# A two-layer spectral and MLP kernel on one core: layer 2's transform over d by frequency modulo four, W left in order, the transform back in halves, copies split by PSUM bank

## The chip, the core and the metric

The kernel runs on one core of one Trainium2 chip. Its engines work side by side, each through its own queue in program order: TensorE (PE; its weight loads are PEld) multiplies into PSUM, VectorE (DVE) and ScalarE (ACT) copy out of PSUM and do the elementwise work, GpSimd (POOL) does small arithmetic on statistics and issues some loads, and SyncE (SP) issues the other DMAs. PSUM has eight banks of 512 fp32 columns. The metric is device microseconds of one launch, the median of several runs.

## The reference

Two layers, each A then B, every one on a normalised input and added back to x, which is 2048 x 512 in bf16.

```
def _A_ref(x, w_r, w_i):
    X = jnp.fft.rfft2(x.astype(jnp.float32), axes=(-2, -1))
    X = X * (w_r + 1j * w_i)
    return jnp.fft.irfft2(X, s=(S, D), axes=(-2, -1)).astype(jnp.bfloat16)

def _B_ref(x, w1, w2, w3, w4):
    h = _gelu(_layernorm(x) @ w1)
    # four column groups of h, moved by 1, -1, 2, -2 rows, zero padded
    x1 = x + shifted(h) @ w2
    return x1 + _gelu(_layernorm(x1) @ w3) @ w4

x = A_x
for _ in range(2):
    x = x + _A_ref(_layernorm(x), A_w_r, A_w_i)
    x = x + _B_ref(_layernorm(x), B_w1, B_w2, B_w3, B_w4)
return x
```

(Here the two layers are written as a loop and the shifts as one name.) D is 512, the hidden width of w3 is 1792.

## The kernel before

The rows are held as s = 16 p + q: 128 partitions p, sixteen row groups q, so that x_state, of 128 x 16 x 512, stays in SBUF for the whole launch. A spectral part goes through these steps, all of them matrix products with tables of sines and cosines:

- *Front* (O, then G): for each q a product over p. The table T is first scaled by the row's 1/std into a tile Tq (Q); TensorE multiplies x_state by it (over_p, over_p_quarters or over_p_plain), and the result is put into V. The sum and the difference of columns d and d+256 serve the even and the odd frequencies; sums of sums and differences of sums serve frequencies 0 and 2 modulo 4. Layer 1's front, over_p_quarters, makes all four parts inside the product, in 8 matmuls a row. Layer 2's front has two ways: for the first PLAIN = 5 pairs of rows, over_p_plain takes 4 matmuls of 128 columns a row and fold_V makes sums and differences on VectorE from the result and from a copy ("right") that ScalarE makes; the others go through over_p, 4 matmuls of 256 columns. Neither makes the sums of sums.
- *Forward*: over_d (d) transforms over d, block by block (16 blocks b, mostly two to a unit u); take_d (t) copies into a tile TV; over_q (q) transforms over q in 64-row matmuls; take_q (x) copies to X, a tile with two buffers; weigh (p) multiplies by the filter W on VectorE; back_q (b) goes back over q, one PSUM bank a block; take_b (m) copies into M, which lies in hT.
- *Back*: back_d (D) goes back over d from all blocks, both halves F of the frequencies summed in one go; take_D (Y) copies; back_p (P) goes back over p; add_x (a) adds to x_state and sums; stats2 (s) squares on ScalarE; rstd2, std_twice, invert_twice and ratio (r, e, i, c) make the scale; norm2 (n) normalises into xn; tr (T) has SyncE transpose xn by DMA into xT.

Layer 1's over_d works with the table FL: two matmuls of 128 columns (frequencies 0 and 2 modulo 4) and two of 256 (the odd ones) a block, and take_d scatters the columns by four. Layer 2's over_d has the table FA and four matmuls of 256 columns a block, with frequencies split by parity only. For that, between the two uses, the filter W is put into even and odd halves: permute (L, sixteen times two copies on VectorE, lines 813 and 814), and G, the table of the way back, is overwritten by G2.

The MLP part is w1 (v), gelu (h), the shifted w2 (u), add_x1 (f), norm (k, R, o), transposes (U), w3 (w), gelu (g), w4 (W), add_x2 (A). In layer 1 it is interleaved with the statistics (B, j, S, J), the scaled tables (Q) and the front of layer 2; in layer 2 with the stores (y).

The order is written out by hand: ORDER_0 for layer 1's front, ORDER_A and ORDER_B for what the two layers do after it. A word such as `d15.7` is operation d on unit 15 with PSUM bank 7 as its first; a last letter A or V names the engine. Every engine runs its own words in the order of the text. `X4.0` is four filler matmuls on zeros in bank 0; WAKE = 27 fillers stand at the start. Loads of weights and tables stand in load_all.

Of the kernel before, what the change touches and what calls it, by code (L numbers as in the profile page):

```python
# [16 lines left out]
P = 128  # L17
# [11 lines left out]
def dft_tables():  # L29
# [27 lines left out]
    FA = np.stack([cos, -sin], axis=1).reshape(2, P, 2, P, 2)[..., ::-1].transpose(1, 0, 4, 2, 3)  # L57
# [8 lines left out]
    G = G.transpose(2, 0, 1)  # L66
    G2 = G.reshape(P, 2, 2, D // 2)
    G = G.reshape(2, P, 2, D // 2).transpose(1, 0, 2, 3)
# [30 lines left out]
    out = {"T": np.stack([T, -T], axis=1), "FA": FA, "FL": FL, "TL": TL, "TL2": TL2, "TR": TR, "G": G, "G2": G2,  # L99
# [9 lines left out]
def kernel(  # L109
# [30 lines left out]
    for last in (False, True):  # L140
        layer(K, last)
        if not last:
            K.load_G2()
# [18 lines left out]
def load_all(K, A_x, A_w_r, A_w_i, B_w1, B_w2, B_w3, B_w4):  # L162
# [29 lines left out]
    def load_tables():  # L192
        spare = K.grp.tile([P, 4, 4, P], BF16, name="xT", bufs=4)
        K.FL = spare[:, 0:2].rearrange("p a b c -> p (a b c)")[:, 0:768]
        K.dummy = spare[:, 2, 0:1]
        q.dma_start(K.FL, dram["FL"])
        load_TL(0)
        load_TL(1)
        load_TR(0)
# [14 lines left out]
    def load_G2():  # L214
        for f in range(2):
            nc.sync.dma_start(K.G[:, f], dram["G2"][:, f])

    K.load_G2 = load_G2

    def load_mlp():  # L220
        gate2 = K.const.tile([1, 16], BF16, name="gate2")
        nc.sync.dma_start(gate2[:], K.W[1:2, 1, NH - 1, 1:17])
        for k in ("G", "Tinv"):
            table(k, nc.sync)
        for k, w, n, c in (("w1", B_w1, 4, D), ("w2", B_w2, 4, D), ("w3", B_w3, 4, FH), ("w4", B_w4, 14, D)):
            t = K.const.tile([P, n, c], BF16, name=k)
            nc.sync.dma_start(t[:], w.rearrange("(t p) n -> p t n", p=P))
            setattr(K, k, t)
        K.FA = K.const.tile(list(tabs["FA"].shape), BF16, name="FA")
        for t in range(2):  # L230
            nc.sync.dma_start(K.FA[:, t], dram["FA"][:, t])

# [48 lines left out]
class Stats:  # L281
# [68 lines left out]
    def invert_twice(self):  # L350
        self.K.nc.vector.reciprocal(self.r[:], self.sd[:])
        self.shift()
# [34 lines left out]
    def apply(self, i, src, dst, eng):  # L387
        r = self.r[:, i:i + 1]
        if eng == "V":
            self.K.nc.vector.tensor_scalar(dst, src, self.mv[:, i, 0:1], r, op0=ALU.add, op1=ALU.mult)  # L390
# [4 lines left out]
def scaled_T(K, q, r, eng="V"):  # L395

    K.Tq[q] = K.stream.tile([P, 2, P], BF16, name="Tq", bufs=12)
# [7 lines left out]
def over_p(K, qs, split=False):  # L405

    ps = banks(K, 2 if split else len(qs))
    for i, q in enumerate(qs):
        Tq = K.Tq.pop(q)
        for t in range(2):  # L410
            o = ps[:, t, 0:256] if split else ps[:, i, t * 256:(t + 1) * 256]
            a, z = t * P, 256 + t * P
            K.nc.tensor.matmul(o, lhsT=K.x[:, q, a:a + P], rhs=Tq[:, 0:1].to_broadcast([P, 2, P]), start=True,
                               stop=False)
            K.nc.tensor.matmul(o, lhsT=K.x[:, q, z:z + P], rhs=Tq[:], start=False, stop=True)
    return ps


def over_p_quarters(K, qs, split=False):

    ps = banks(K, 2 if split else len(qs))
    for i, q in enumerate(qs):
        T = K.Tq.pop(q)
        plus, both, swap = T[:, 0], T[:], T[:, ::-1]
        twice = lambda k: T[:, k:k + 1].to_broadcast([P, 2, P])
        for h in range(2):
            o = (ps[:, h, 0:256] if split else ps[:, i, h * 256:(h + 1) * 256]).rearrange("d (k p) -> d k p", k=2)
            terms = ((0, o, twice(0)), (1, o[:, 1], plus), (3, o[:, 1], plus), (2, o, swap)) if h == 0 else \
                    ((1, o, swap), (0, o[:, 0], plus), (2, o[:, 0], plus), (3, o, twice(1)))
            for n, (c, dst, rhs) in enumerate(terms):  # L430
                K.nc.tensor.matmul(dst, lhsT=K.x[:, q, c * P:(c + 1) * P], rhs=rhs, start=(n == 0), stop=(n == 3))  # L431
    return ps
# [13 lines left out]
def fold_V(K, qs, ps, right):  # L446
    n, lo = len(qs), qs[0]
    v = K.V[:].rearrange("d (t h) b q c -> d h t q b c", h=2)[:, :, :, lo:lo + n]
    left = ps[:, :, 0:256].rearrange("d q (t b c) -> d t q b c", t=2, c=4)
    right = right.rearrange("d q (t b c) -> d t q b c", t=2, c=4)  # L450
    for h, op in ((0, ALU.add), (1, ALU.subtract)):
        for t in range(2):
            K.nc.vector.tensor_tensor(v[:, h, t], left[:, t], right[:, t], op=op)


def take_V(K, qs, ps, eng, part=False):

    dst = K.V[:].rearrange("d t b q c -> d (t b) q c")[:, :, qs[0]:qs[-1] + 1:max(qs[-1] - qs[0], 1)]
    if part:
        t = "AV".index(eng)  # L460
        dst, ps = dst[:, 64 * t:64 * t + 64], ps[:, t:t + 1, 0:256]
    copy(K, dst, ps.rearrange("d q (tb c) -> d tb q c", c=4), eng)
# [7 lines left out]
def first_front(K):  # L470
# [30 lines left out]
    def front(k):  # L501
        ps[k] = over_p_quarters(K, FIRST[k], k == len(FIRST) - 1)
# [3 lines left out]
    def take(k, eng):  # L506
        take_V(K, FIRST[k], ps[k], eng, k == len(FIRST) - 1)

    def means(g):
# [3 lines left out]
        if g == TABLES:  # L513
# [3 lines left out]
             "J": lambda g: L[g].invert(), "p": lambda g: L[g].rstd(), "Q": scale, "O": front, "G": take}  # L517
    for op in ORDER_0.split():
        if op[0] in "QG":
            table[op[0]](int(op[1:-1]), op[-1])  # L520
        else:
            table[op[0]](int(op[1:]))
    K.load_rest(last_T[:])
    K.load_mlp()
    K.nc.sync.dma_start_transpose(K.dummy, K.zeros[:])


def layer(K, last):
# [13 lines left out]
    def over_d(u):  # L542
        bs = UNITS[u]
        ps["d", u] = o = banks(K, len(bs))
        for i, b in enumerate(bs):
            if not last:
                oi = o[:, i].rearrange("p (e r f) -> p e r f", e=2, r=4)
                part = lambda k: V[:, k, 2 * b:2 * b + 2].rearrange("d b q c -> d (b q c)")
                nc.tensor.matmul(oi[:, :, 3], lhsT=part(1), rhs=K.FL[:, 0:P].rearrange("p (e f) -> p e f", e=2),
                                 start=True, stop=True)  # L550
                nc.tensor.matmul(oi[:, :, 1], lhsT=part(2), rhs=K.FL[:, P:2 * P].rearrange("p (e f) -> p e f", e=2),
                                 start=True, stop=True)
                for k in range(2):
                    rhs = K.FL[:, (k + 1) * 256:(k + 2) * 256].rearrange("p (e r f) -> p e r f", e=2, r=2)
                    nc.tensor.matmul(oi[:, :, 0:3:2], lhsT=part(3 * k), rhs=rhs, start=(k == 0), stop=(k == 1))
                continue
            oi = o[:, i].rearrange("p (e h f) -> p h e f", e=2, h=2)
            for h in range(2):
                for t in range(2):
                    nc.tensor.matmul(oi[:, 1 - h], rhs=K.FA[:, t, h],  # L560
                                     lhsT=V[:, 2 * t + h, 2 * b:2 * b + 2].rearrange("d b q c -> d (b q c)"),
                                     start=(t == 0), stop=(t == 1))

    def take_d(u, eng):
        n = len(UNITS[u])
        tv[u] = K.stream.tile([P, n, 512], BF16, name="TV", tag="TV_Y", bufs=4, padded_shape=[P, 2, 512])
        src = ps.pop(("d", u))
        if last:
            copy(K, tv[u][:], src, eng)
        else:  # L570
            copy(K, tv[u][:].rearrange("p n (e f r) -> p (n e) f r", e=2, r=4),
                 src.rearrange("p n (e r f) -> p (n e) f r", e=2, r=4), eng)
# [14 lines left out]
    def take_q(u, eng):  # L587
        n = len(UNITS[u])
        X[u] = K.stream.tile([P, 4, 256], BF16, name="X", bufs=2)
# [3 lines left out]
    def weigh(u):  # L593
        n = len(UNITS[u])
        small = n == 1 and u not in LATE[last]
        k = n_pab[small]
        n_pab[small] += 1
        if small:
            t = PB[k % 2][:, 6].rearrange("p (l h) f -> p l h f", l=2)
        else:  # L600
            t = PB[k % 2][:, 2 * (k % 6 // 2):2 * (k % 6 // 2) + 2, 0:2 * n]
        pab[u] = t
        nc.vector.tensor_tensor(t, X.pop(u)[:, 0:2 * n].unsqueeze(1).to_broadcast([P, 2, 2 * n, 256]),  # L603
                                K.W[:, :, 2 * u:2 * u + 2 * n, 1:257], op=ALU.mult)

    def back_q(b):
        u = [u for u in UNITS if b in UNITS[u]][0]
        both = TAKE_B[last][b] == "B"
        ps["b", b] = o = banks(K, 1 + both)
        for F in range(2):  # L610
            for h in range(2):
                oh = o[:, F, h * P:(h + 1) * P] if both else o[:, 0, (2 * h + F) * P:(2 * h + F + 1) * P]
                for k in range(2):
                    nc.tensor.matmul(oh,  # L614
                                     lhsT=pab[u][:, k, 2 * (b - u) + h, F * P:(F + 1) * P],
                                     rhs=K.TR[:, k:k + 2, 2 * b + h], start=(k == 0), stop=(k == 1))

    def take_b(b, eng):
        dst = M[:, :, :, :, b * 8:b * 8 + 8].rearrange("f F e q (h c) -> f h (F e) q c", h=2)
        if TAKE_B[last][b] == "B":  # L620
            F = "VA".index(eng)
            dst, src = dst[:, :, 2 * F:2 * F + 2], ps["b", b][:, F, 0:256]
        else:
            src = ps["b", b][:, 0]
        copy(K, dst, src.rearrange("f (h g q c) -> f h g q c", h=2, q=NQ, c=4), eng)

    def back_d(m):
        ps["D", m] = o = banks(K, 2)
        for F in range(2):
            for i in range(2):  # L630
                for e in range(2):
                    nc.tensor.matmul(o[:, i, e * 256:(e + 1) * 256], lhsT=M[:, F, e, 2 * m + i, :], rhs=K.G[:, F, e, :],  # L632
                                     start=(F == 0 and e == 0), stop=(F == 1 and e == 1))
# [4 lines left out]

    def back_p(q):
        ps["P", q] = o = banks(K, 1)[:, 0]  # L640
        y = Y[q // 2][:, q % 2]
        for h, e, c in ((0, 0, 0), (0, 1, 0), (1, 0, 0), (1, 1, 1)):
# [289 lines left out]
```

## Time and profile before

| | |
|---|---|
| median of 3 runs | 347.33 us (347.32 to 347.7) |
| span of the profiled execution | 345.6 us, 5672 instructions |
| granted TensorE clock | 1.00 throughout |
| HBM read and written | 12.13 MB and 2.10 MB, 41 GB/s over the span |
| w3 matmuls (L735), 448 of 512 columns | 99.3 us |
| w4 matmuls (L755) | 98.3 us |
| layer 2's over_d (L560), 64 of 256 columns | 7.7 us |
| layer 1's over_d (L549, L551, L555), 16 + 16 + 32 | 3.5 + 3.5 + 5.6 us, partly side by side |
| copies that permute W (L813, L814) | 11.0 + 6.9 us |
| fold_V (L453), 20 of 256 columns | 7.0 us |

Busy times are unions: where a matmul is drawn as 272 ns and the next starts 109 ns later, the two overlap in the record. What a matmul costs its queue is therefore read from start to start, not from its own length. Windows are counted from the start of the span.

### The profile page before, as it was taken

The numbers are of one execution on the slowest core, as the hardware profiler recorded it, in microseconds if no ns is written. First come the engines' busy times: TensorE is split into PE (matmuls) and PEld (weight loads), VectorE is DVE, ScalarE is ACT, GpSimd is POOL, SyncE is SP. The second block draws the span as 40 slices with busy tenths as digits, with TensorE's granted clock in tenths as the row PEclk, the third lists the DMA queues.
The fourth block names the chain that finished last, engine by engine and source line by source line (L and its number), as shares of the span: only waits on it lengthen the run. The fifth ranks groups of instructions, "written<-read, shape, count | busy, mean of one in ns | idle before, by whom it ended". The sixth has DMA issues, their size and how long they took to land.

```text
span 345.6 us, 5672 instructions
## 1 busy us (share of the span) xinstructions
PE 336.6 (97%) x2161; PEld 190.3 (55%) x2178; DVE 187.5 (54%) x448; ACT 195.5 (57%) x348; POOL 62.8 (18%) x157
## 2 busy tenths in 40 slices
PE   6999999999999999999999999999999999999996
PEld 4978884444444444444577888544444444444443
DVE  5989597668354351178789969757514110211021
ACT  4989899755616616015527979976572344132500
POOL 1460047530301400010000002554014001000000
PEclk9999999999999999999999999999999999999999
DMA  7997975430031210300000002572103060203012
GB/s 259 280 361 236 383 173 101 84 62 0 3 61 21 33 24 14 49 13 1 2 0 2 2 2 44 99 97 41 27 2 61 0 108 0 46 14 95 0 32 76
DMA packets 45834, 25.12 MB, mean 73 GB/s; under 512 B 35008, under 2 KB 42816, under 8 KB 45808
## 3 DMA queue, kind: packets, MB, share of 16 engines
q1 hardware_dynamic: 44336, 20.27, 24.8%
q0 software_dynamic: 1232, 4.40, 3.7%
q8 instruction: 17, 0.28, 0.4%
q10 hardware_dynamic: 240, 0.10, 0.1%
q14 instruction: 9, 0.07, 0.1%
HBM read 12.13 MB, written 2.10 MB: 41 GB/s over the span
## 4 chain that ended last, share of the span: by engine, by line
PE 83%; ACT 7%; DVE 5%; DMA 3%; issue 2%; SPq 0%; ACTq 0%; DVEq 0%
PE ps L735 28%; PE ps L755 28%; PE ps L700 8%; PE ps L684 7%; PE ps L431 3%; PE ps L632 2%; PE ps L614 2%; ACT xn L306 2%; PE ps L644 1%; ACT hT L159 1%; DVE PB L603 1%; PE ps L584 1%; ACT X L159 1%; DVE X L157 1%; DVE x_state L652 1%
## 5 line engine op out<-in xcount | busy, mean ns | idle before, releaser
L742 ACT ACTIVATE gT<-ps 128x1024 bf16<-128x1024 f32 x56 | 56.6, 1023 | 80.4 <-PE ps L735 79.7
L735 PE MATMUL ps<-xT,w 128*128 128x512 bf16 x448 | 99.3, 379 | 0.0
L755 PE MATMUL ps<-w,gT 128*128 128x512 bf16 (+1 forms) x464 | 98.3, 366 | 0.6
L755 PEld LDWEIGHTS <-gT 128*128 128x128 bf16 x476 | 46.5, 98 | 50.1
L735 PEld LDWEIGHTS <-w 128*128 128x128 bf16 x448 | 43.8, 98 | 52.6
L761 DVE TENSOR_TENSOR x_state<-ps,x_state 128x512 bf16<-128x512 f32 (+1 forms) x34 | 22.1, 657 | 86.1 <-PE ps L755 78.9
L708 DVE SCALAR_TENSOR_TENSOR xn<-xn,ln_c,ps 128x512 bf16<-128x512 bf16 x32 | 23.5, 745 | 26.3 <-PE ps L700 19.5
L700 PE MATMUL ps<-w,hT 128*128 128x512 bf16 x123 | 28.8, 379 | 0.3
L684 PE MATMUL ps<-xT,w 128*128 128x512 bf16 x128 | 28.8, 379 | 0.2 <-DMA xT<-xn 0.2
L306 ACT ACTIVATE junk<-xn 128x512 bf16<-128x512 bf16 x32 | 19.9, 622 | 12.7 <-DVE xn L708 12.7
L652 DVE SCALAR_TENSOR_TENSOR x_state<-ps,x_state 128x512 bf16<-128x512 f32 x32 | 20.5, 686 | 4.2 <-PE ps L644 4.1
L294 DVE BATCH_NORM_STATS2 ln_st<-x_state 128x6 f32<-128x512 bf16 (+1 forms) x31 | 20.1, 663 | 3.7 <-DMA x_state<-in_A_x_dram 3.5
L700 PEld LDWEIGHTS <-hT 128*128 128x128 bf16 x128 | 12.4, 98 | 15.3 <-ACT hT L691 0.8
L684 PEld LDWEIGHTS <-w 128*128 128x128 bf16 x128 | 12.3, 98 | 15.3 <-DMA xT<-xn 1.4
L312 POOL TENSOR_SCALAR ln_mv<-ln_s 128x4 f32<-128x4 f32 x16 | 5.7, 357 | 80.3 <-DVE x_state L652 68.7
L306 ACT ACTIVATE xn<-x_state 128x512 bf16<-128x512 bf16 x32 | 20.0, 631 | 0.4 <-DVE x_state L652 0.2
L603 DVE TENSOR_TENSOR PB<-X,W 128x2048 bf16<-128x2048 bf16 (+1 forms) x20 | 19.4, 1010 | 0.2
L691 ACT ACTIVATE hT<-ps 128x512 bf16<-128x512 f32 x32 | 17.4, 604 | 2.5 <-PE ps L684 2.4
L314 POOL TENSOR_TENSOR ln_mv<-ln_s,ln_t 128x4 f32<-128x4 f32 x16 | 3.8, 239 | 80.1 <-ACT junk L306 73.5
L614 PE MATMUL ps<-TR,PB 128*128 128x128 bf16 x256 | 16.3, 219 | 0.1
L159 ACT ACTIVATE TV<-ps 128x1024 bf16<-128x1024 f32 (+1 forms) x16 | 14.2, 914 | 3.8 <-PE ps L560 2.3
L644 PE MATMUL ps<-Y,Tinv 128*128 128x256 bf16 x128 | 15.4, 272 | 0.5 <-ACT Y L159 0.2
(96 smaller groups left out, 388.3 us busy)
## 6 DMA issues: line engine op xcount, KB each, us to landing
w<-in_B_w_dram SPq DMA_DIRECT2D x2, 1792.0 KB, 13.0
W<-W POOLq DMA_DIRECT2D x4, 514.0 KB, 4.7
x_state<-in_A_x_dram SPq DMA_DIRECT2D x8, 256.0 KB, 4.5
out_dram<-x_state SPq DMA_DIRECT2D x15, 128.0 KB, 1.8
w<-in_B_w_dram SPq DMA_DIRECT2D x2, 512.0 KB, 4.8
W<-in_A_w_r_dram SPq DMA_DIRECT2D x7, 128.5 KB, 6.9
W<-in_A_w_i_dram SPq DMA_DIRECT2D x7, 128.5 KB, 6.6
TL<-tab_TL POOLq DMA_DIRECT2D x3, 256.0 KB, 5.1
```

What stands on the lines that cost most here:

```text
L159: K.nc.scalar.activation(dst, src, ACT.Copy, bias=0.0, scale=1.0)
L306: K.nc.scalar.activation(out, src, ACT.Square, bias=0.0, scale=D ** -0.5, accum_out=self.s[:, i, 1:2])
L603: nc.vector.tensor_tensor(t, X.pop(u)[:, 0:2 * n].unsqueeze(1).to_broadcast([P, 2, 2 * n, 256]), K.W[:, :, 2 * u:2 * u + 2 * n, 1:257], op ...
L614: nc.tensor.matmul(oh, lhsT=pab[u][:, k, 2 * (b - u) + h, F * P:(F + 1) * P], rhs=K.TR[:, k:k + 2, 2 * b + h], start=(k == 0), stop=(k == 1))
L652: nc.vector.scalar_tensor_tensor(K.x[:, q, :], ps.pop(("P", q)), 1.0, K.x[:, q, :], op0=ALU.mult, op1=ALU.add, accum_out=ln[g].s[:, i, 0:1])
L684: nc.tensor.matmul(o[:, i], lhsT=K.w1[:, t, j * P:(j + 1) * P], rhs=xT[g][:, :, t, :], start=(t == 0), stop=(t == 3))
L700: nc.tensor.matmul(o, lhsT=K.hT[:, j, st:st + P], rhs=K.w2[:, j, :], start=(j == 0), stop=(j == 3))
L708: nc.vector.scalar_tensor_tensor(xn[:, q, :], xn[:, q, :], ln[q // 4].c[:, q % 4:q % 4 + 1], ps.pop(("u", n)), op0=ALU.mult, op1=ALU.add, ...
L735: nc.tensor.matmul(o[:, i], lhsT=K.w3[:, c, t * P:(t + 1) * P], rhs=xT3[g][:, :, c, :], start=(c == 0), stop=(c == 3))
L742: nc.scalar.activation(gT[g][:, 2 * j:2 * j + 2, :], ps.pop(("w", k)), ACT.Gelu_apprx_tanh, bias=0.0, scale=1.0)
L755: nc.tensor.matmul(o, lhsT=gT[g][:, t, i * P:(i + 1) * P], rhs=K.w4[:, t, d], start=(t == 0), stop=(t == 13))
L761: nc.vector.tensor_tensor(x, ps.pop(("W", n)), x, op=ALU.add)
```

## The change

The four-part form of V, FL and the untouched W and G now serve both layers. Layer 2's over_d takes layer 1's four matmuls; FA, G2, permute and over_p are gone, and FL has a tile of its own. Layer 2's fold_V writes the two odd parts and a tile "pairs" of sums, and fold_again makes the other two parts from it. Six pairs of rows go the plain way in place of five; pair 6 and the single rows 14 and 15 go through over_p_quarters. That function now gives one PSUM bank to each half of d and interleaves the rows of a pair in it, so that a copy can take one bank (words G and L for the halves 0 and 1).

On the way back, back_q and take_b of blocks 12 to 15 are split by F into two banks (b and V, m and l), and back_d into its two halves (D and C). X has three buffers, Tq eight in place of twelve. shift is taken out of invert_twice (M). The additions of resid, the products of weigh and the scaling of Tq can name an engine. half_D and fold_D are added; FOLD, which selects them in back_p, is empty, and the words K and H are in no order. All three orders are new; their stages are given below where they begin and end.

```diff
@@ over_p_quarters
-    ps = banks(K, 2 if split else len(qs))
+    n = len(qs)
+    ps = banks(K, 2)
     for i, q in enumerate(qs):
         T = K.Tq.pop(q)
-        plus, both, swap = T[:, 0], T[:], T[:, ::-1]
+        plus, both, swap = [v.rearrange("d k (b c) -> d k b c", c=4) for v in (T[:], T[:], T[:, ::-1])]
...
         for h in range(2):
-            o = (ps[:, h, 0:256] if split else ps[:, i, h * 256:(h + 1) * 256]).rearrange("d (k p) -> d k p", k=2)
+            o = ps[:, h, 0:256 * n].rearrange("d (k b q c) -> d k b q c", k=2, q=n, c=4)[:, :, :, i]
             terms = ((0, o, twice(0)), (1, o[:, 1], plus), (3, o[:, 1], plus), (2, o, swap)) if h == 0 else \
                     ((1, o, swap), (0, o[:, 0], plus), (2, o[:, 0], plus), (3, o, twice(1)))
@@ fold_V
-    for h, op in ((0, ALU.add), (1, ALU.subtract)):
-        for t in range(2):
-            K.nc.vector.tensor_tensor(v[:, h, t], left[:, t], right[:, t], op=op)
+    for t in range(2):
+        K.nc.vector.tensor_tensor(v[:, 3 * t], row(ps[:, :, 0:256])[:, t], row(right)[:, t], op=ALU.subtract)
+    K.nc.vector.tensor_tensor(pairs, ps[:, :, 0:256], right, op=ALU.add)
+def fold_again(K, qs, pairs, eng):
+    n, lo = len(qs), qs[0]
+    e = K.nc.vector if eng == "V" else K.nc.gpsimd
+    row = pairs.rearrange("d q (t b c) -> d t q b c", t=2, c=4)
+    v = K.V[:].rearrange("d t b q c -> d t q b c")[:, :, lo:lo + n]
+    for t, op in ((1, ALU.add), (2, ALU.subtract)):
+        e.tensor_tensor(v[:, t], row[:, 0], row[:, 1], op=op)
@@ take_V
-    copy(K, dst, ps.rearrange("d q (tb c) -> d tb q c", c=4), eng)
+    if half is not None:
+        dst, ps = dst[:, 64 * half:64 * half + 64], ps[:, half:half + 1]
+    copy(K, dst.rearrange("d (h z) q c -> d h z (q c)", z=64), ps.rearrange("d h (z x) -> d h z x", z=64), eng)
@@ over_d (layer 1's branch, now for both layers)
-            oi = o[:, i].rearrange("p (e h f) -> p h e f", e=2, h=2)
-            for h in range(2):
-                for t in range(2):
-                    nc.tensor.matmul(oi[:, 1 - h], rhs=K.FA[:, t, h],
+            nc.tensor.matmul(oi[:, :, 3], lhsT=part(1), rhs=K.FL[:, 0:P].rearrange("p (e f) -> p e f", e=2),
+                             start=True, stop=True)
+            nc.tensor.matmul(oi[:, :, 1], lhsT=part(2), rhs=K.FL[:, P:2 * P].rearrange("p (e f) -> p e f", e=2),
+                             start=True, stop=True)
+            for k in range(2):
+                rhs = K.FL[:, (k + 1) * 256:(k + 2) * 256].rearrange("p (e r f) -> p e r f", e=2, r=2)
+                nc.tensor.matmul(oi[:, :, 0:3:2], lhsT=part(3 * k), rhs=rhs, start=(k == 0), stop=(k == 1))
@@ take_q
-        X[u] = K.stream.tile([P, 4, 256], BF16, name="X", bufs=2)
+        X[u] = K.stream.tile([P, 4, 256], BF16, name="X", bufs=3)
@@ back_d
-    def back_d(m):
-        ps["D", m] = o = banks(K, 2)
-        for F in range(2):
-            for i in range(2):
+    def back_d(m, F):
+        if F == 0:
+            ps["D", m] = banks(K, 2)
+        o = ps["D", m]
+        for i in range(2):
@@ constants
-WAKE = 27
+WAKE = 30
-TAKE_B = ("FFFFFFFFFFFFFFFB", "FFFFFFFFFFFFFFFB")
+SPLIT_B = ((12, 13, 14, 15), (12, 13, 14, 15))
+SPLIT_FIRST = (5, 6, 7, 8)
+SPLIT_V = (6, 14, 15)
-PLAIN = 5
+PLAIN = 6
+FOLD = [(), ()]
@@ ORDER_0: start and end
-s0 s1 s3 i1 i0 s2 s4 i3 i2 S0 J0 Q0V s5 i4 S1 J1 Q1A O0 s6 s7 i6 i7 s8 Q2A Q3A O1 f2 S2 J2 i8 Q6V Q7V s9 f3 s10 O3 Q4V
+s1 s0 i1 i0 s3 S0 s2 s5 J0 Q1A Q0A s7 i2 i3 s4 S1 J1 O0.4 s9 f2 s6 Q2V i7 i4 i6 s10 Q3A O1.0 S2 J2 G0A Q4V s11 s8 Q5A
...
-J5 Q14V O5 Q15V O6 G5V O7 G7A G6V O8 G8A G8V
+Q13V O6.6 L5A i15 S5 J5 Q15V O8.4 Q14V G4A G6A L6A O7.2 G7A L7A G1V G8V L8V
@@ ORDER_A: the end of layer 1's forward part, and the turn to layer 2
-b13.5 m9V b14.1 m12A b15.2 m13A m14A X4.0 m15A m15V D1.5 Y1A D0.0 Y0A D3.3 Y3A P2.5 a2 s2 P3.6 a3 s3 P0.0 a0 P7.2 s0
+p15V b12.7 b13.2 m12A b8.6 b15.5 m11V V15.1 m13A V13.7 m8A m14V m15V V14.2 l15V D0.4 l12V l13A l14V D1.6 C1 Y1A C0
...
-j13 S13 Q12 W24.4 A24 B24 J13 Q13 W14.5 A14 B14 O4.6 O15.2 G4A j14 S14 G15A G15V O5.4 G5A O6.1 J14 Q14 O14.3 G6A G4V
-X3.5 G14V X4.0 G14A L7
+I4V W12.6 A12 B12 W13.3 W15.7 j12 S12 J12 A13 B13 j13 W24.3 S13 Q12V J13 Q13V A15 B15 W14.1 j15 A24 O5.2 B24 S15 J15
+A14 B14 j14 Q15V G5A S14 O6.0 J14 O15.4 G6A Q14A O14.6 L6A L15A G14A G5V I5V G15A L14A
@@ ORDER_B: layer 2's forward part and the start of its way back
-d15.7 t15V d4.1 t4V d1.3 t1A d8.6 q1.4 x1V t8A p1 q4.2 x4A q15.0 x15V p4 d12.4 t12A d10.6 q8.2 p15 q12.4 t10A b1.0
...
+X5.0 d15.0 t15V d1.3 d4.4 d12.0 t4A q15.6 t1V x15A d8.2 q4.4 t12V q1.6 t8A d2.0 p15V x1V b15.2 t2V p1V d0.3 x4A q12.6
+d10.4 m15A t0A q0.0 x12A q2.2 t10A p4V b1.6 x0V p0V m1A d6.4 p12V q8.0 b4.6 x2A d14.7 t14V q10.2 t6A q6.4 b5.7 m4A
+b13.6 x8A p2V x10A p8V p10V b0.1 b2.0 x6A m2A b3.2 m3A q14.4 p6V x14A b9.3 p14V b8.0 b12.2 m0A b10.4 V13.5 b11.1 m13A
+b7.6 m9A m12A m5V b14.2 b6.3 V12.7 m8A V14.0 m11V m10A m14A m6A V15.1 l15A m7V D3.2 l13A D2.4 l12V l14V C3 C2 D1.6 Y2V
+C1 Y3A P7.1 a7 P6.0 a6 Y1A D0.2 s7 C0 Y0A s6 P4.1 a4 s4 P5.7 a5 P2.6 P3.1 s5 a3 s3 r1 D4.2 P0.7 a2 P1.1 s2 D7.4 a0 C7
```

## The prediction

> **What bounds the kernel.** I read the page's head first, then the trace cut into stages at the points where the chain of waits changes its line, then that chain around layer 2's spectral part, and last the rows of single matmuls.
>
> ```profile
> PE 336.6 (97%) x2161; PEld 190.3 (55%) x2178; DVE 187.5 (54%) x448; ACT 195.5 (57%) x348; POOL 62.8 (18%) x157
> ```
>
> TensorE is called busy for 97%, but ends of matmuls are modelled, so short holes do not show. The stages (window, its length, then busy time of PE, PEld, DVE, ACT, POOL):
>
> ```profile
> 8.20:19.50 11.30, 10.89 (x129) 9.74 (x128) 11.16 (x36) 10.09 (x21) 6.55 (x13) 1.00 0.98 308
> 19.50:38.05 18.55, 18.41 (x260) 15.13 (x260) 17.00 (x22) 17.38 (x27) 3.36 (x6) 1.00 0.90 307
> 38.05:52.50 14.45, 14.26 (x129) 12.56 (x130) 10.87 (x33) 13.27 (x29) 4.34 (x15) 1.00 0.81 235
> 52.50:178.70 126.20, 125.78 (x616) 59.25 (x622) 72.38 (x186) 61.80 (x108) 24.59 (x54) 1.00 0.18 32
> 178.70:182.95 4.25, 4.18 (x41) 3.39 (x39) 3.99 (x13) 3.38 (x6) 0.00 (x0) 1.00 0.00 0
> 182.95:202.80 19.85, 19.17 (x257) 16.39 (x258) 18.75 (x23) 17.04 (x26) 0.00 (x0) 1.00 0.01 2
> 202.80:217.40 14.60, 14.31 (x128) 12.46 (x129) 11.71 (x32) 12.59 (x28) 2.25 (x10) 1.00 0.20 38
> 217.40:342.40 125.00, 124.25 (x583) 57.58 (x590) 37.43 (x95) 56.70 (x98) 20.59 (x52) 1.00 0.23 44
> ```
>
> They are: front of layer 1; its spectral forward part; its way back; its MLP with most of layer 2's front; the turn between the layers; forward and back of layer 2; its MLP. In the MLPs VectorE and ScalarE are about half idle or more, so only TensorE's own instructions count. In the two forward stages three engines are nearly full, and a copy that is late shows. The chain of waits says where it does in layer 2:
>
> ```profile
> 182.96 2.79 PE ps L560 x24
> ...
> 188.33 1.75 DVE PB L603 x2
> ...
> 197.03 4.87 PE ps L614 x80
> ...
> 202.42 0.39 ACT hT L159
> 202.80 1.90 PE ps L632 x16
> ```
>
> TensorE stands from its last back_q matmul (202.1) until the last copy into hT has ended (202.8), since back_d reads every block.
>
> I measure TensorE by pitch, from start to start: 0.109 us for 256 columns, 0.056 for 128, 0.216 for 512, 0.061 for a 64-row matmul of over_q and for the 128x(2x64) ones of back_q. Forward, layer 2: 64 x 0.109 + 64 x 0.061 + 128 x 0.061 = 18.7 us of the 19.85, so 1.15 us of waits. Forward, layer 1: 16 x 0.33 + 3.9 + 7.8 = 17.0, plus 0.44 of filler, in 18.55: 1.1 of waits.
>
> **The d transform of layer 2.** The rows of the old and the new form stand side by side, as layer 1 already runs the new one:
>
> ```profile
> 20.01 0.22 PE L549 MATMUL ps<-xT,V 128*128 128x128 bf16 x1
> 20.34 0.22 PE L549 MATMUL ps<-xT,V 128*128 128x128 bf16 x1
> 182.96 2.79 PE L560 MATMUL ps<-FA,V 128*128 128x256 bf16 x24
> ```
>
> A block costs 0.33 us in layer 1 (20.01 to 20.34) and 4 x 0.109 = 0.44 in layer 2. Sixteen blocks: **-1.7 us**, on a path where TensorE is the fullest engine. The copy out now scatters by four: layer 1's rows of that form take 0.69 us on VectorE for 512 columns and about 1.04 on ScalarE for 1024, layer 2's plain ones 0.68 and 1.02, so nothing.
>
> Does the rest of the stage let it through? By pitch (ScalarE 0.92 per 1024 columns, 0.50 per 512, 0.30 for 256; VectorE 1.13, 0.58, 0.33; weigh 1.17 and 0.60) the new order has 16.7 us on ScalarE and 16.2 on VectorE beside 17.0 on TensorE. I walked the new order engine by engine. Counted from the start of d15: d10 ends near 6.0, but ScalarE still has t0 and x12 ahead of t10, which runs from 6.8 to 7.75; d6 wants that bank and TensorE is ready at 7.3, a wait of 0.5. x6 ends at 13.2, and q14 behind it could start at 12.95: 0.25. b6 ends at 17.15, m6 runs until 18.1, TensorE is free at 17.85: 0.25 before D3. A few changes to and from over_q lose 0.14 each (so they do now). About 1.15 in all, as now. So 18.15 against 19.85: **-1.7**. The three X buffers and the split copies work inside this sum: each of blocks 12 to 15 pays 2 x 0.30 for 0.50 on ScalarE, 0.4 us a layer, and in exchange back_d's first half starts before the last copies of the second half.
>
> **Layer 1 forward.** The same walk gives 18.05 for 18.55: the four filler matmuls go and the last wait shortens: **-0.5**. The doubled W rows do not decide: their last landing was 28.5 and p14 needs them near 33; q10 falls within 0.1 us of the landing of the second table half (24.6, or 25.0 as its gate moves with the last Tq).
>
> **Front of layer 2.** Pair 5 becomes plain: 8 x 0.056 = 0.45 in place of 8 x 0.109 = 0.87. Pair 6 and rows 14 and 15 go from 4 to 8 matmuls a row: 4 x 0.109 + 4 x 0.056 = 0.66 for 0.44. One pair more lies ahead of the last w4 (five in place of four): **+0.45** in the MLP, not hidden. In the turn TensorE has 0.45 + 4 x 0.66 = 3.1 plus 0.55 of filler; before it was 3.1 plus 0.76. There the chain decides: last w4, A14 0.45, B14 0.45, j14 0.23, S14 0.3, J14 0.16, now Q14 on ScalarE (0.49, was 0.26 on VectorE) behind G6, O14 0.66 (its first half is copied while the second runs), then G14, G15, L14 at 0.30: 4.36 with the latencies between them (0.02 to 0.25 each in the old chain), against 4.23, **+0.1**. Q15 on VectorE now stands behind A14, B14 and j14 and is ready 1.4 us after the last w4; O15, which waits for it, has its turn on TensorE at 1.75. The fold in two steps costs VectorE 0.72 + 0.69 + 0.74 for 1.41, +0.74 a pair; for five pairs the MLP hides it, for pair 5 it ends at 3.95 beside the 4.36.
>
> **Removed and hidden.** Permuting W: L813 and L814, 11.0 + 6.9 us of VectorE. Nearly all lies in the MLP, where VectorE had 72 of 126 us: 0 there; the last pair (182.6 to 183.7) stood ahead of the first TV copies, which I count as nothing since d15 ended then too. FA and G2 loads: hidden, 0. resid, weigh and scaled_T got an engine letter, but no order names GpSimd; half_D and fold_D are in no order, so these parts of the change do nothing. The one-element table loads z0 go from both orders: 0.2 us of ScalarE each, hidden.
>
> **Front of layer 1.** Both first Tq go to ScalarE behind the sums of row 5, but the first two statistics stand first: S0 at 5.9 (was 6.48), row 5 until 7.3, Q1, Q0 until 8.24: first matmul 8.3 for 8.19. Then 64 x 0.109 + 64 x 0.056 = 10.4 with little waiting, the last copies in halves on ScalarE until 19.4: start of d0 as now, **0**, +-0.4. Here a rule speaks against the change. The matmuls of over_p_quarters now write PSUM in runs of four fp32, a row of stride eight. The Trainium skill, Advanced Engine Details and Errata, PSUM Cachelines, warns that an access pattern that is not contiguous slows matmuls significantly, and asks that each two neighbours be contiguous. The nearest row, L549, writes two runs of 64 with a gap and keeps 0.056 us, and L644, which reads its moving operand backwards, 0.109. Sum by the rows: 0. By the rule's first sentence, with doubling as my estimate, the front's 10.4 and the turn's 2.6 would grow by 13 us; by its last sentence runs of four are harmless. I take 0; the ends are 0 and +13.
>
> **The ways back.** Same matmuls, in two halves. Layer 1: the walk has T0 and T1 leave near 9.5 and 11.2 us after D, as now (9.2, 11.1), and a transpose took 3.0 to 3.2: 0. Layer 2: before, e1 came 8.7 us after D and v at 14.6, when its transpose landed (217.3); now e1 near 9.0 as D2 stands behind l13: **+0.25**. Bound for each: -0.5 (all its waits gone) to +0.6. The MLPs had no holes but missing records; a badly placed gelu could cost, which I put at 0 to +0.5, value 0.
>
> **Sum:** -1.7 - 0.5 + 0.45 + 0.1 + 0 + 0 + 0.25 = -1.4 us on the span of 345.6. The runs show 347.33, 1.8 above it for what lies around the span; that stays. **345.9 us.**
>
> **Rivals.** Two tenths of a per cent, 0.7 us, is what a measurement can tell from no change.
> 1. Forecast, 345.9, own range 345.2 to 346.6: chance 0.50.
> 2. *The waits go too.* Holes by pitch: 0.5 front, 1.1 and 1.15 forward, 0.5 and 0.7 back, 0.3 at the start of MLP 2, near 4.2 in all. If the new orders take 1.5 more of them: 344.4. For it: split copies and halves attack just these. Against: three engines stay nearly full. 0.22.
> 3. *ScalarE becomes the bound of layer 2's forward stage.* At 16.7 of 17.0 it has no slack; if TensorE, coming sooner, waits 1.2 us more, the stage gives 0.5 only: 347.1. For it: ScalarE is busy without a hole from t4 to t10 in my walk. 0.17.
> 4. *Slower: strided PSUM writes.* In 128 matmuls of layer 1's front and 32 of the turn, 13 us. It decides from 11% upwards (13 x 0.11 = 1.4); at 25%: +3.2, 349.1. Against: L549's row. 0.11.
>
> Faster: 0.46 + 0.22 + 0.03 = 0.71. Same: 0.04 + 0.10 = 0.14. Slower: 0.04 + 0.11 = 0.15. The range 343.8 to 347.6 leaves out rival 4 and the ends of the others.
>
> **What would show it.** Right: in layer 2 the first three d matmuls' group at 0.33 a block and the forward stage at 18 to 18.4; no hole of 0.6 before D3; turn 4.2 to 4.5. Rival 4: starts of L431's successors more than 0.109 and 0.056 apart. Rival 3: more waits of PE for banks that ScalarE holds. Wrong: holes inside an MLP, or v of layer 2 later than 15.2 us after D.

## The result, and the profile after

| | before | after |
|---|---|---|
| median of 20 runs each, side by side | 347.49 us (347.0 to 348.69) | 346.49 us (345.92 to 347.5) |
| ratio after / before | | 0.9965, 95% interval 0.9955 to 0.9974 |
| span of the profiled execution | 345.6 us | 345.0 us |

The change makes the kernel 1.0 us faster by these medians. In 29 of the 92 runs of before beside the kernels below, the granted clock is 0.994 or 0.995 and the time 1.4 us longer than in the rest; six of the twenty here, from 348.28 us on, lie near those and none of after's does, and without these six before's median is 347.31 and the gain 0.8. The head of the page after:

```profile
PE 337.0 (98%) x2191; PEld 188.2 (55%) x2191; DVE 175.8 (51%) x421; ACT 197.4 (57%) x361; POOL 60.8 (18%) x157
```

VectorE lost 11.7 us of busy time (187.5 before), mostly the permutation of W, and no stage shows it: it had stood beside matmuls. The stages say where the time went. These are four of the eight windows of the trace after, cut at the first matmul of each stage (layer 1 forward, MLP 1, the turn, layer 2 forward); the columns are window, length, then busy time of PE, PEld, DVE, ACT and POOL:

```profile
...
19.65:38.15 18.50, 18.24 (x257) 14.28 (x258) 16.90 (x22) 17.49 (x29) 4.14 (x7) 1.00 0.86 285
...
52.60:179.30 126.70, 126.70 (x632) 59.80 (x631) 63.36 (x166) 60.95 (x107) 22.89 (x55) 1.00 0.16 30
179.30:183.35 4.05, 3.91 (x47) 3.30 (x45) 3.39 (x10) 3.24 (x9) 0.00 (x0) 1.00 0.00 0
183.35:202.05 18.70, 18.14 (x257) 14.36 (x256) 17.39 (x22) 16.87 (x28) 0.00 (x0) 1.00 0.01 2
...
```

In the forward stages VectorE and ScalarE are each busy for over nine tenths (before too, but for ScalarE in layer 2, 17.04 of 19.85); in MLP 1 VectorE went from 72.4 to 63.4 us. Read from the first matmul of a stage to the first of the next, to 0.01 us:

| stage | before | after | change | forecast |
|---|---|---|---|---|
| until the first matmul | 8.19 | 8.77 | +0.58 | +0.1 |
| front, layer 1 | 11.29 | 10.87 | -0.42 | -0.1 |
| forward, layer 1 | 18.57 | 18.49 | -0.08 | -0.5 |
| back, layer 1 | 14.40 | 14.48 | +0.08 | 0 |
| MLP 1 | 126.27 | 126.71 | +0.44 | +0.45 |
| turn | 4.23 | 4.04 | -0.19 | +0.1 |
| forward, layer 2 | 19.83 | 18.70 | -1.13 | -1.7 |
| back, layer 2 | 14.65 | 14.59 | -0.06 | +0.25 |
| MLP 2 | 124.70 | 124.65 | -0.05 | 0 |
| behind the last matmul | 3.43 | 3.75 | +0.32 | 0 |

The eight stages between first and last matmul lose 1.41 us, and the forecast's terms for them sum to 1.5, with terms that are off in both directions. The first row depends on the execution: the first rows of x landed 4.84 us into this one, and 3.88 to 4.30 us into seven of the kernels below that load the same things in the same order, whose first matmul came at 7.81 to 8.24 (probe had them at 4.15, a later row late, and 8.77 again). The last row, +0.32, is the same in those seven within 0.02 us; what it comes from stays open.

The largest gain is layer 2's forward stage, and it is smaller than forecast. The chain of waits after, in that stage (start, us, what):

```profile
191.59 0.60 ACT hT L154
192.18 0.91 ACT X L154
193.10 0.80 ACT TV L154
193.89 0.61 ACT hT L154
194.51 1.21 ACT X L154 x2
195.71 0.46 issue
196.18 0.88 ACT X L154
197.08 1.16 ACT hT L154 x2
198.24 0.49 ACT X L154
198.73 3.29 ACT hT L154 x7
202.06 1.93 PE ps L612 x16
```

Before, the middle and the late part of this chain had been PE L614 for 4.87 us in one piece and DVE for 1.75. After, it runs over ScalarE from 191.6 to 202.06: ten and a half microseconds of one copy behind the other. This says whose work ended last, not what a shorter copy would be worth; light_m below takes 1.8 us out of this stretch and gains 0.44. On the page the share of ScalarE in the whole chain rises from 7% to 12% and that of PE falls from 83% to 80%:

```profile
PE 80%; ACT 12%; DMA 3%; DVE 2%; issue 2%; SPq 0%; ACTq 0%; DVEq 0%
```

### The profile page after: what moved, and what is told of

Same layout as the page of the kernel before. It is cut to its first block, busy times and chain, and to the rows that moved or that the text cites. A ratio compares the mean times of both kernels' runs of the same rounds, so it can differ in the third digit from the quotient of the medians.

```text
span 345.0 us, 5696 instructions
## 1 busy us (share of the span) xinstructions
PE 337.0 (98%) x2191; PEld 188.2 (55%) x2191; DVE 175.8 (51%) x421; ACT 197.4 (57%) x361; POOL 60.8 (18%) x157
## 4 chain that ended last, share of the span: by engine, by line
PE 80%; ACT 12%; DMA 3%; DVE 2%; issue 2%; SPq 0%; ACTq 0%; DVEq 0%
PE ps L751 28%; PE ps L731 28%; PE ps L696 8%; PE ps L680 7%; PE ps L403 3%; ACT hT L154 3%; ACT xn L290 3%; ACT X L154 3%; ACT Y L154 2%; PE ps L612 1%; ACT TV L154 1%; DMA T<-tab_T 1%; DMA x_state<-in_A_x_dram 1%; PE ps L550 1%; DMA xT<-xn 1%
## 5 line engine op out<-in xcount | busy, mean ns | idle before, releaser
L738 ACT ACTIVATE gT<-ps 128x1024 bf16<-128x1024 f32 x56 | 55.8, 1022 | 87.8 <-PE ps L731 78.1
L290 ACT ACTIVATE junk<-xn 128x512 bf16<-128x512 bf16 x32 | 19.8, 622 | 3.2 <-DVE xn L704 3.2
L640 PE MATMUL ps<-Y,Tinv 128*128 128x256 bf16 x128 | 16.1, 272 | 0.4 <-ACT Y L154 0.3
L612 PE MATMUL ps<-G,hT 128*128 128x256 bf16 x128 | 15.6, 273 | 0.3 <-ACT hT L154 0.2
L592 PEld LDWEIGHTS <-PB 128*128 128x128 bf16 x256 | 14.7, 98 | 2.1 <-issue 1.5
```

Of the source, the lines that this page charges most:

```text
L290: K.nc.scalar.activation(out, src, ACT.Square, bias=0.0, scale=D ** -0.5, accum_out=self.s[:, i, 1:2])
L592: nc.tensor.matmul(o[:, k0 * P:(k0 + 1) * P], lhsT=pab[u][:, k, 2 * (b - u) + h, f * P:(f + 1) * P], rhs=K.TR[:, k:k + 2, 2 * b + h], star ...
L738: nc.scalar.activation(gT[g][:, 2 * j:2 * j + 2, :], ps.pop(("w", k)), ACT.Gelu_apprx_tanh, bias=0.0, scale=1.0)
```

## The experiments

A stage's length is read as in the table above. Ratios are to the kernel before, run beside each kernel.

### Which engine sets the pace of the new forward stage

My theory was that TensorE still sets most of it and that the rest of the forecast gain fell to ScalarE's copies; the rivals were ScalarE alone, and VectorE with its products. One kernel makes each engine's work heavier or lighter by itself.

**long_d** makes layer 2's two 128-column d matmuls of a block 256 wide again (the result is then not the transform):

```diff
@@ over_d
+            if last:
+                nc.tensor.matmul(o[:, i, 0:256], lhsT=part(1), rhs=K.FL[:, 0:256], start=True, stop=True)
+                nc.tensor.matmul(o[:, i, 256:512], lhsT=part(2), rhs=K.FL[:, 0:256], start=True, stop=True)
```

> The changed kernel with layer 2's two 128-column d matmuls of each block made 256 columns long, as long as those of the kernel before (their result is not the transform): 1.7 us more on TensorE in layer 2's forward stage, all copies and orders as they are. Theory 1 (TensorE sets the pace): the stage grows from 18.7 to 20.4 us and the launch by 1.7. Theory 2 (ScalarE's copies set the pace, TensorE waits in any case): it grows by 0.4 to 1.1, to 19.1 to 19.8.

Measured: 347.8 us (347.51 to 348.43), ratio 1.0004, 0.9993 to 1.0015. The stage took 20.01 for 18.70: +1.31 of the 1.7 us put in, between the two theories. Behind the first matmul, all other stages stayed within 0.04 of after's.

**light_m** copies half of the columns in layer 2's nine whole-block copies that ScalarE makes into hT; the other half is left out:

```diff
@@ take_b
+        if last and F is None and eng == "A":
+            dst, src = dst[:, :, 0:2], src[:, :, 0:2]
```

> The changed kernel with the nine whole-block copies into hT that ScalarE makes in layer 2's forward stage cut to half their columns (the rest of hT keeps old values): some 1.8 us less on ScalarE. Theory 2 (ScalarE sets the pace): the stage falls from 18.7 to 17.5 to 18.1 us, the launch by 0.6 to 1.2. Theory 1 (TensorE, or VectorE's products) : the stage stays within 0.2 of 18.7.

Measured: 346.0 us (345.92 to 346.83), ratio 0.9945, 0.9924 to 0.9966. The stage took 18.26: -0.44 for 1.8 us taken from ScalarE, again between the theories. Most of it is one hole of TensorE, ahead of q14, where it waits for a bank until ScalarE has copied it to X: 0.38 us in after, 0.05 here. The hole ahead of back_d stays at 0.39.

**light_p** leaves the multiplication by W out of layer 2's products; VectorE copies X instead:

```diff
@@ weigh
+        if last:
+            nc.vector.tensor_copy(t, xb)
+        else:
+            nc.vector.tensor_tensor(t, xb, K.W[:, :, 2 * u:2 * u + 2 * n, 1:257], op=ALU.mult)
```

> The changed kernel with layer 2's products by W replaced by plain copies of X (the multiplication is left out): about 0.6 us in place of 1.17 for two blocks, 4 to 4.5 us less on VectorE in layer 2's forward stage. If VectorE is among what sets the pace there, the stage falls from 18.7 to 17.8 to 18.3; if ScalarE and TensorE alone do, it stays within 0.2.

Measured: 346.4 us (345.92 to 347.04), ratio 0.9958, 0.9946 to 0.9971. Groups of that stage in light_p and in after (line, engine, operation, shapes, count, then busy us and mean ns, then idle time ahead of it):

```profile
L583 DVE COPY PB<-X 128x2048 bf16<-128x2048 bf16 (+1 forms) x10 | 5.7, 582 | 1.6 <-ACT X L154 1.6
```
```profile
L581 DVE TENSOR_TENSOR PB<-X,W 128x2048 bf16<-128x2048 bf16 (+1 forms) x10 | 9.6, 1008 | 0.0
```

VectorE has 3.9 us less to do, and the stage takes 18.70 as before: the time turns up as 1.6 us in which VectorE waits for ScalarE's X. VectorE, busy for 17.39 of the 18.70 us in after and so the fullest engine but TensorE, costs nothing.

Together: TensorE passes on three quarters of what it is given (1.31 of 1.7), ScalarE a quarter of what is taken from it (0.44 of 1.8, in its copies into hT), VectorE none of 3.9. The busy shares (18.1, 16.9, 17.4 us) would have ranked them differently.

What keeps the stage from giving the whole 1.7 us is in TensorE's own order. Its starts show that a visit to over_q costs about 0.2 us beyond its matmuls, in both kernels. Here is one visit before (16 matmuls) and one after (8):

```profile
186.86 1.91 PE L560 MATMUL ps<-FA,V 128*128 128x256 bf16 x16
188.70 1.05 PE L584 MATMUL ps<-TV,TL 64*128 64x256 bf16 x16
189.68 0.51 PE L614 MATMUL ps<-TR,PB 128*128 128x128 bf16 x6
```
```profile
188.55 0.38 PE L550 MATMUL ps<-FL,V 128*128 128x256 bf16 x2
188.86 0.61 PE L568 MATMUL ps<-TV,TL 64*128 64x256 bf16 x8
189.40 0.23 PE L544 MATMUL ps<-FL,V 128*128 128x128 bf16 x1
```

Within a visit two 64-row matmuls start 0.003 us apart and a pair every 0.109, so 0.0545 each. Before: 186.86 + 16 x 0.109 = 188.60, but over_q starts at 188.70; 188.70 + 16 x 0.0545 = 189.57, but back_q starts at 189.68. After, by the same count, 0.09 us go in and 0.10 out. Before has four visits in this stage and after seven. Taken apart by the starts (matmuls at 0.109 for 256 columns, 0.056 for 128 and for back_q, 0.0545 for over_q; the small rest left out), layer 2's forward stage is:

| kernel | matmuls | visits to over_q | other holes over 0.03 us | stage |
|---|---|---|---|---|
| before | 17.6 | 4: 0.8 | 1.4 | 19.83 |
| after | 15.9 | 7: 1.4 | 1.2 | 18.70 |
| long_d | 17.6 | 7: 1.4 | 0.9 | 20.01 |
| light_m | 15.9 | 7: 1.4 | 0.8 | 18.26 |
| light_p | 15.9 | 7: 1.4 | 1.2 | 18.70 |
| fl_alone (below) | 15.9 | 4: 0.8 | 2.5 | 19.33 |

The other holes are mostly waits for copies. The new order has less of them than the old order with the same transform (1.2 for 2.5) and pays 0.6 us for it in visits. Whether fewer visits would keep the waits short was not tried.

**rebal** tries to use that VectorE's load costs nothing here and that ScalarE's costs a little: one of ScalarE's copies goes to VectorE, and one of VectorE's products to GpSimd, which does nothing in this stage. In ORDER_B:

```diff
-... x0V p0V m1A ... V14.0 m11V m10A m14A ...
+... x0V p0P m1A ... V14.0 m11V m10V m14A ...
```

> A version meant to be faster: in layer 2's forward stage the product of unit 0 goes to GpSimd, which is idle there, and one copy of 512 columns (m10) from ScalarE to VectorE. VectorE keeps its load, ScalarE has 0.5 us less. If copies share the pace with TensorE as the lighter copies showed (0.44 us for 1.8): the stage falls by 0.1 to 0.3 us, the launch to about 346.3. If GpSimd's product (1.5 to 2.5 us by its other rows) is late for b0: it grows by up to 0.5.

Measured: 346.97 us (346.53 to 348.96), ratio 0.9991, 0.9976 to 1.0006; the stage took 19.35, so +0.65. The timeline of GpSimd, and ScalarE's wait for it:

```profile
191.28 2.78 POOL L581 TENSOR_TENSOR PB<-X,W 128x1024 bf16<-128x1024 bf16 x1 [34.17 <-ACT TV L154]
```
```profile
ACT X L154 <- POOL PB L581: 0.4, 1, 0.4
```

A one-block product takes 2.78 us on GpSimd; the 1024-column form takes 0.68 on VectorE. It holds its X buffer that long, ScalarE's next copy to X waits 0.4, and the wait lies on the chain of that run. Of the 0.65, a hole of TensorE between two back_q matmuls has 0.53 (0.61 for 0.08) and the one ahead of back_d 0.14 (0.52 for 0.38). Cheap in one engine's free time is not cheap where a buffer is held meanwhile. Moving m10 alone was not tried.

### What the three X buffers and the split copies are worth

**x2** takes the third X buffer away (`name="X", bufs=3` to `bufs=2`).

> The changed kernel with two X buffers in place of three. If the third buffer carries the new orders, each forward stage grows by 0.3 to 1.0 us (copies x wait for the product two units earlier); if not, both stay within 0.1 of 18.5 and 18.7.

One run: 349.56 us (before: 347.59). Forward stages 19.93 and 20.16, for 18.49 and 18.70: +1.44 and +1.46, more than the range expected. Waits that after does not have at all:

```profile
ACT X L154 <- PE ps L550: 0.7, 1, 0.7
PE ps L592 <- DVE PB L581: 0.4, 1, 0.4
```

**whole_b** copies blocks 12 to 15 whole (`SPLIT_B = ((), ())`, the words V and l gone from both orders).

> The changed kernel with blocks 12 to 15 of back_q copied whole again (one bank and one copy each, back_d still in two halves): 0.1 us less per block of copying, but back_d's first half waits for the last whole copies. If the split helps: both forward stages, up to the first back_d, grow by 0.2 to 0.6 us. If it only moves work: within 0.1.

One run: 348.38 us (before: 347.43). Forward stages 19.31 and 19.56: +0.82 and +0.86, again above the range. The hole ahead of the first back_d matmul grows from 0.38 to 1.07 us in layer 2 (from 0.25 to 1.11 in layer 1), since back_d's first half now waits for the second half's copies too:

```profile
PEld L612 <- ACT hT L154: 1.1, 1, 1.1
```

So these two parts, which the forecast had only inside its sum, carry 1.45 and 0.85 us in each layer of an order that was written for them; what they would give to the old orders was not tried. In one run each, the new order without one of them is slower than the kernel before.

### The transform alone

**fl_alone** is the kernel before with the four-part transform and nothing else: FL for both layers, no permutation, five operations in fold_V, the single rows and the later pairs of layer 2's front through over_p_quarters, the L words taken out of otherwise old orders.

```diff
@@ front of layer 2
-        ps["O", k] = over_p_plain(K, qs) if k < PLAIN else over_p(K, qs, k >= 14)
+        ps["O", k] = over_p_plain(K, qs) if k < PLAIN else over_p_quarters(K, qs, k >= 14)
@@ over_d
-            if not last:
+            if True:
```

> The kernel before with one part of the change alone: layer 2 takes the four-part d transform with FL, W and G stay as they are, permuting and its copies go; all orders, banks, copies and PLAIN = 5 as before, over_p replaced by the quarter form in the turn, the fold in five VectorE operations at once. The turn should grow by about 1.2 us on both theories (24 matmuls of 0.109 become 24 of 0.109 and 24 of 0.056, and the fold of pair 4 takes 0.7 us more). Theory 1 (TensorE's own instructions set the pace of layer 2's forward stage): that stage falls by 1.7 us to about 18.1, the launch by 0.5 us (ratio 0.9985). Theory 2 (the copies out of PSUM set it): it falls by 0.5 to 1.0, to 18.8 to 19.3, and the launch grows by 0.2 to 0.7 us (ratio 1.0005 to 1.002).

Measured: 349.18 us (348.5 to 350.38), ratio 1.0041, 1.0025 to 1.0058: **slower than before**. Forward, layer 2, took 19.33, so only 0.50 of TensorE's 1.7 us came out; its holes other than visits grew from 1.4 to 2.5 us and took the rest (the largest are 0.62, 0.57 and 0.62 us; before has none, 0.25 and 0.62 at these places). The turn took 5.30 (+1.07): all its rows pay 8 matmuls, with nothing moved out of it. And MLP 2 took 125.70 (+1.00), which no part of the edit touches:

```profile
219.05 3.62 PE L677 MATMUL ps<-xT,w 128*128 128x512 bf16 x16
223.83 1.47 PE L677 MATMUL ps<-xT,w 128*128 128x512 bf16 x6 [1.17 <-DMA xT<-xn]
```

In this timeline TensorE stands 1.17 us between two groups of w1, for a transpose. The next experiments are about that.

### The stall that moves with the number of instructions

The two transposes that w1 waits for landed 4.8 us after their issue in fl_alone, and 3.3 in after. The DMA view of fl_alone from the issue of the first to its landing (busy tenths of the 16 DMA engines in 40 slices, what moved, and the median time to landing):

```profile
DMA  9999720000799999999998999990000000000099
...
q1 hardware_dynamic: 2364, 0.59, 95.2%
q8 instruction: 1, 0.02, 1.8%
...
xT<-xn SPq DMA_TRANSPOSE x2, 4.8
```

And that of after for the same two, where the only packet of an "instruction" queue is one of 8 KB ("q14", "0.01" MB):

```profile
DMA  9961000000299999999994699999999992000000
...
q14 instruction: 1, 0.01, 0.5%
...
xT<-xn SPq DMA_TRANSPOSE x2, 3.3
```

In fl_alone a 16 KB packet of the queue called "instruction" falls into it (at 220.3 us, 1.50 us long; below I call it a fetch), packets of the transpose take up to 1.72 us where the median is 0.02, the DMA engines fall silent (the zeros late in the row), and the landing is 1.5 us late. Every kernel here has 17 such packets (probe 18), some 16 KB for each 130 matmuls with their weight loads, which is what a fetch of TensorE's own instructions would look like. If so, the place of the stall is set by how many instructions lie ahead of it, and the edit matters only as it changes that number. Two kernels shift it with fillers at the start alone, holding the time that the fillers take:

**fl_shift**: fl_alone with 14 wake fillers of 512 columns for 27 of 256.

```diff
-WAKE = 27
+WAKE = 14            (and WAKE_COLUMNS = 4: fillers of 4 x 128 columns)
```

> The part alone (fl_alone: old orders, four-part transform in layer 2) with its 27 waking fillers of 256 columns replaced by 14 of 512, 26 instructions fewer ahead on TensorE. Theory F: the fetch at 220.5 comes 2 to 3 us later, after the two transposes have landed; the hole of 1.3 us between the w1 groups shrinks to 0.3 and the launch is 0.8 to 1.0 us shorter than fl_alone's (349.18). If the fetch does not matter: the hole stays.

Measured: 348.74 us (347.66 to 350.57), ratio 1.0032, 1.0015 to 1.0049. The fetch now comes at 223.3, the two transposes land 3.2 and 3.3 us after issue, and MLP 2 takes 124.35, as it should: the hole is gone. But the whole gains only 0.4 us, not the 0.8 to 1.0 expected, because MLP 1 went from 126.26 to 127.39. There a fetch at 65.4 now falls behind the issue of a transpose (64.84; it lands after 3.75 us), the next one is issued 2.6 us later in place of 1.3, and TensorE stands there instead:

```profile
PE ps L678 <- DMA xT<-xn: 0.9, 1, 0.9
```

**after_shift**: after with 60 wake fillers of 128 columns for 30 of 256 (`WAKE = 60`, `WAKE_COLUMNS = 1`).

> The changed kernel with its 30 waking fillers of 256 columns replaced by 60 of 128: the same time at the start, 60 more instructions (30 matmuls, 30 weight loads) ahead of everything else on TensorE. Theory F (a 16 KB fetch of TensorE's instructions that falls on the transposes holds them up): the fetch at 221.5 comes some 5 us earlier, near 216, onto the transposes of xn that w1 of row groups 0 to 3 waits for; they land 4.5 to 5 us after their issue in place of 3.3, w1 waits 1.0 to 1.6 us, and the launch is 1.0 to 1.6 us longer than that of the changed kernel (346.49). If the fetch does not matter: within 0.3 of it.

Measured: 348.27 us (347.76 to 350.21), ratio 1.0024, 1.0004 to 1.0044: 1.8 us above after's 346.49, and slower than before, by thirty more fillers of half the size. Its first matmul is no later (8.02). The fetch moves from 221.3 to 217.0, into the transpose that the first w1 group waits for; that chain, from its issue on (start, us, what):

```profile
214.27 4.77 DMA xT<-xn
219.04 0.05 issue
219.08 5.37 PE ps L681 x24
```

In after the same transpose took 3.19 us (213.34 to 216.53). The hole ahead of w1 is 1.51 us in the matmul starts, which is the 1.51 that the stage "back, layer 2" gains (16.10 for 14.59). In this execution layer 1's forward stage was 0.85 longer as well, behind a table half that landed at 26.93 (25.47 in after); whether the shift has to do with that stays open.

So the stall appears, goes and changes its place with the number of TensorE instructions ahead of it. That the 16 KB packets are TensorE's own instructions is inferred from their number. In the profile of before the fetch fell at 224.7, on the next pair of transposes (landed 4.6 and 4.0 us after issue), for which no matmul was waiting; in after at 221.3, 0.2 us ahead of the issue of a pair that took 3.15 and 3.04. Neither paid.

The traces of all twelve kernels bound this. Of 276 transposes of xn that no instruction packet touches, none took more than 3.35 us. Of 33 in which a 16 KB packet starts between issue and landing, 16 took 3.4 to 5.0 us and 17 stayed within 3.34; of 52 with one of 8 KB alone, 16 took 3.7 to 4.2; where a 16 KB packet had started ahead of the issue (23), none was late. So a packet inside the transpose was there whenever one was late, but it does not always make it late; what decides that was not found.

fl_alone without its collision would be near 349.18 - 1.33 (the hole, by starts) = 347.85, 0.4 above before and within what theory 2 had: in the old orders the algebra by itself wins nothing, and its -0.5 us in the forward stage is more than paid back in the turn.

### Strided PSUM writes

**probe** puts 16 contiguous fillers and 64 matmuls of 256 columns ahead of layer 2's first d matmul, the latter with their fp32 results in runs of 64, 4, 2 and 1 with equal gaps between (16 of each):

```diff
+    for run in (64, 4, 2, 1):
+        for _ in range(16):
+            o = K.ps[:, 0, :].rearrange("d (b q c) -> d b q c", q=2, c=run)[:, :, 0]
+            K.nc.tensor.matmul(o, lhsT=K.zeros[:], rhs=..., start=True, stop=True)
```

> The changed kernel with 80 filler matmuls of 256 columns in place of five at the start of layer 2: 16 contiguous, then 16 each that write PSUM in runs of 64, 4, 2 and 1 fp32 with a gap of the same length after each run. If only the number of columns counts: 0.109 us from start to start in all five groups. If a pattern that is not contiguous is slow in itself: the groups from 64 on above 0.12. If pairs are what counts: runs of 64, 4 and 2 at 0.109, runs of 1 near 0.21. The stage starts about 8 us later.

One run, 359.7 us, read for its pitches alone. The timeline: contiguous ones first, then the 64:

```profile
182.69 1.91 PE L270 MATMUL ps<-zeros 128*128 128x256 bf16 x16
184.44 8.86 PE L264 MATMUL ps<-FL,zeros 128*128 128x256 bf16 x64
```

Start to start a matmul takes 0.109 us contiguous and in runs of 64, 4 and 2, and 0.216 in runs of 1: 3 x 16 x 0.109 + 16 x 0.216 = 8.7, the 8.86 of the row less the tail of the last one. Runs of one cost exactly double, runs of two nothing.

## Why the forecast came out as it did

- **The d transform of layer 2 (-1.7).** TensorE's own part is right: a block costs 0.33 us, and its work in the stage fell by 1.7. The step that failed is "Does the rest of the stage let it through?": the walk put the waits at "about 1.15 in all, as now", and they are 1.7 (18.70 less the 17.0 of work). So 1.13 came out, not 1.7; the stage ended outside the 18 to 18.4 given as its sign. The copies that the walk named are right in sum: it had holes of 0.5, 0.25 and 0.25 us at d6, q14 and D3, and the starts show 0.16, 0.38 and 0.38. The mis-sized term is "A few changes to and from over_q lose 0.14 each (so they do now)". The new order has seven visits where the old one has four, at 0.2 us each: 0.6, about all that is missing. The pitch of 0.061 hid it: sixteen over_q matmuls in a row with the way out take 0.98 us, 0.061 each, but four take 0.325, 0.081 each.
- **Rival 3, ScalarE as the bound,** did not come, though the stage ended between forecast and rival. Its sign shows once, in the 0.38 us ahead of q14 for a bank that ScalarE holds; but TensorE's holes other than visits went from 1.4 to 1.2 us in all. By light_m a quarter of a change in ScalarE's copies reaches the stage.
- **The split copies and the third X buffer** stood inside the sum as a small trade (0.4 us for an earlier start). The trade is right in sign, and taking either part out of the new order costs far more than that price: 0.85 us a layer for the split, 1.45 for the buffer.
- **Layer 1 forward (-0.5).** -0.08. The four fillers went (0.44) and other holes fell from 1.1 to 0.8 us, but TensorE visits over_q eight times in place of five: 0.6 us. It is the same term of the walk.
- **MLP 1 (+0.45).** Right to 0.01: matmuls moved ahead of the last w4 have no cover.
- **The turn (+0.1).** -0.19. Each step of the chain was in the list; the sum was 0.3 too long. The walk let d15 wait for the copies G14, G15 and L14; its first matmul (183.36) follows the second of them, and L14, drawn from 183.17 to 183.58, is waited for only by the next matmul, in a hole of 0.22 us that counts to the forward stage.
- **Front of layer 1 (0).** Right for the start of d0: 18.8 to 19.8 over the kernels with the new orders, 19.48 before. The rule weighed there fell by its first sentence: runs of four are free in probe (0.109 us), as its last sentence has it. Rival 4 is out.
- **Back, layer 2 (+0.25).** -0.06: v came 14.59 us behind D, one pitch behind the last back_p matmul, so the later e1 cost nothing; the transpose that v needs landed at 216.53, as that matmul started. MLP 2 (0): -0.05, though by luck of where the fetch fell.
- **Rival 2 (1.5 us more of the waits go)** did not come: in the forward stages the waits for copies fell by 0.2 and 0.3 us, and the visits to over_q took 0.6 in each.

The sum was met better than its terms, and that is luck. The forward stages gave 1.0 us less than forecast (0.57 and 0.42), and the front, the turn and layer 2's way back 0.9 more.

## What to carry to other kernels

When one engine's work in a full stage is cut, expect the others to take back a part of it, and find out which by making each heavier or lighter in turn: the busy shares named VectorE here, and it was free. Count also what the fullest engine pays for changing between kinds of work: a pitch read from long runs is too small for short ones. A buffer or a split that unties two engines can be worth more than the arithmetic saved; in the old orders the arithmetic alone gained nothing. And where a change moves a stage that it doesn't touch by a microsecond, look at what the instruction queues fetched during the slow transfer before explaining it.

## What was not expected of the hardware

An instruction packet that falls into a DMA transpose can hold it up: 4.7 and 4.9 us from issue to landing in fl_alone and 4.8 in after_shift, for 3.0 to 3.35 undisturbed. Where TensorE waits for it, that is 1.1 to 1.5 us of a 347 us kernel, more than the whole change brought, and thirty fillers at the start can decide whether it falls there. A change from 128-row matmuls to pairs of 64-row ones cost TensorE 0.1 us and the change back another 0.1, in every visit shown here. And a matmul's PSUM write pays for gaps only when no two neighbours are together: 0.109 us in runs of two, 0.216 in runs of one.
